# Four reordering casts of a weight matrix, shared among three engines instead of one

## The chip, the cores and the metric

The kernel runs on one core of a Trainium2 chip. The core has five engines with a queue of instructions each, run in order: PE (matrix multiply, with weight loads shown as PEld), ACT (ScalarE), DVE (VectorE), POOL (GpSimd) and SP (SyncE, which here only issues transfers). They work side by side and wait for each other through semaphores. The metric is the time of one execution on the device, in microseconds (us).

## The reference

A gated linear attention over 4 batches, 8 heads, 768 tokens and a head size of 48 gives `x` of 3072 tokens by 384; two matrix products with a gate between them follow.

```python
f = 1.0 / (1.0 + np.exp(-f_logit))
for t in range(S):
    state = f[:, :, t, :, None] * state + np.einsum('bhd,bhe->bhde', k[:, :, t], v[:, :, t])
    y[:, :, t] = np.einsum('bhd,bhde->bhe', q[:, :, t], state)
...
h = x @ w_in            # w_in: 384 x 2048
g = h * np.cos(h)
return (g @ w_out).astype(np.float32)   # w_out: 2048 x 384
```

Inputs and output are float32.

## The kernel before

**Two halves.** The attention is done in 12 pairs of 128-token chunks (256 tokens a pair, three pairs a batch). The products are done in 13 units `m` of tokens: units 0 and 1 have 128 tokens (together the first pair), the other eleven have 256. Unit 2 is the second pair.

**Steps of a pair `n`.** Loads `f`, `k`, `q`, `v` (SP, some ACT); `ex`, `ln`, `fx`, `fy` make decays from `f_logit` on ACT; `qa`, `ka`, `qm`, `km` scale q and k on POOL; `ad` adds two decays (POOL); `cum` sums them on PE and `eb`, `ei` take exponents on ACT; `vb` and `vt` lay out v; `tq`, `tk` turn q and k on PE and `qkt` copies them; `sc` are the scores (PE, L461), `am` masks them (DVE, L465); `ps`, `st`, `sz` carry the state (PE, DVE); `y` and `yi` are the outputs (PE, L535); `xe` copies each into `x` (ACT or DVE).

**Steps of a unit `m`.** `h{m}.{j}{s}` multiplies x by a part of w_in (PE, L583) into a pair of PSUM banks, `co{m}.{j}` takes the cosine on ACT (L588, its own activation table), `g{m}.{j}` multiplies the two on DVE (L565) into a tile `g`, `o{token tile}.{s}` multiplies `g` by a quarter of w_out (PE, L599), `ot` and `out` copy and store. A unit of 128 tokens has two `j`, one of 256 tokens four.

**The weights.** Each of w_in and w_out comes in four pieces of 768 KB. `w{part}.{i}` fetches a piece as float32 into a slot of the tile pool `g`, which is the same pool that the gates write to; `wc{part}.{i}` casts it to bf16 into its final place. For w_in (part 0) the cast also reorders: column 4n + r of a piece goes to place 128r + n, since w_out is fetched with four neighbouring rows on a partition (L281). Per partition that is 3 rows of 512 elements, 1536 in all. Each of the four casts reads one float out of four, with a step of 16 bytes, and writes in a row. The w_out casts copy in a row on both sides.

Slots of `g` set waits: w0.3 is fetched into the slot of w0.0, so it waits for wc0.0; w1.1 follows in the same slot and waits for wc0.3; w1.3 waits for wc1.1. The gates g1.* go to the slot of w0.1 and g2.* to that of w0.2, so they wait for wc0.1 and wc0.2. h0.00 and h1.00 need wc0.0; h1.01, h0.01 and h2.1* need wc0.1; h2.2*, h1.10 and h0.10 need wc0.2; h2.3*, h1.11 and h0.11 need wc0.3.

**Order.** Every engine's order comes from one list of words, `ORDER` (L36 to L117). `wc0.0:G` says that step wc0.0 runs on POOL at this place; T, S, V, G, Y stand for PE, ACT, DVE, POOL and SP, and numbers behind are the places of new tiles (of PSUM banks T0 to T7 for matmuls). Nothing is reordered later. ACT changes its activation table between the exponent group (L641) and the cosines (L588). The first 51 matmuls, by zeros (L264), stand among the first attention steps and write nothing that is used.

Of the kernel before, what the change touches and what calls it, by code (L numbers as in the profile page):

```python
# [15 lines left out]
B, H, S, D = 4, 8, 768, 48  # L16
# [14 lines left out]
         "sz": 4, "x": 4, "g": 5, "co": 4, "ot": 4}  # L31
WITHIN = 12
ZEROS = 51


ORDER = """  # L36
# [11 lines left out]
zf45:T4 vt0.3:S zf46:T0 qm1.0:V zf47:T1 zqk.0:V vb1:G1 cum3:T6 ka1.1:V tk1.0:T7 am0.1:V0 eb3:S1  # L48
tq1.0:T km1.1:G ps1.0:T0,1 qkt1.0:S3 zf48:T4 zf49:T4 zf50:T4 qa1.1:V ps1.1:T vt1.1:G2 vt1.3:S
sc1.0:T2 zsp.2:V qm1.1:V y0:T7 ex2:S st1.00:V q3:Y1 tq1.1:T4 am1.0:V0 tk1.1:T w0.2:Y3 ei3:S0 ln2:S0  # L50
qkt1.1:V4 wc0.0:G vt1.2:S sz1.00:V0 xe0.1:S0 st1.01:V xe0.0:S sz1.01:V sc1.1:T4 ad2:G2 w0.3:Y1
vt1.0:S yi1:T0,3 am1.1:V2 fx2:S k3:Y2 h0.00:T6 fy3:S w1.0:Y2 wc0.1:G cum2:T2 y1:T ei2:S1 xe1.0:S1
h1.00:T4 xe1.1:V qa3:G eb2:S0 h1.01:T st1.11:V st1.10:V qm3.1:G2 h2.00:T2 sz1.11:V3 sz1.10:V h0.01:T
co1.0:S2 qm3.0:G h2.01:T co0.0:S0 wc0.2:G q2:Y1 g1.0:V4 h2.11:T0 h2.10:T co2.0:S1 g0.0:V0 wc0.3:G
h2.20:T4 co2.1:S2 h2.21:T g2.0:V3 h1.10:T6 ka3:G w1.1:Y1 co2.2:S3 f5:Y2 h1.11:T g2.1:V km3.0:G fy2:S
h0.10:T2 k2:S0 h0.11:T wc1.0:G g2.2:V co1.1:S0 h2.31:T0 co0.1:S1 g1.1:V h2.30:T qa2:G w1.2:Y2
o0.0:T5 v2:Y0 co2.3:S3 zsz.2:V qm2.1:G1 g0.1:V o1.0:T6 o2.0:T4 qm2.0:G wc1.1:S g2.3:V tq3.1:T7
# [131 lines left out]
def describe(nc, cpool, ppool, q, k, v, f_logit, moe_w_in, moe_w_out, out):  # L189
    G = Graph()  # L190
    eng = lambda e: {"DVE": nc.vector, "POOL": nc.gpsimd, "ACT": nc.scalar, "SP": nc.sync}[e]

    def tl(shape, dt, name):
        return cpool.tile(shape, dt, name=name)

    def copy(e, o, i):
        (nc.scalar.copy if e == "ACT" else eng(e).tensor_copy)(out=o, in_=i)  # L197


    if ZEROS:  # L200
        zero = tl([128, 512], BF16, "zero")
# [57 lines left out]

    if ZEROS:  # L260
        for i in range(ZEROS):
            dump = Val(p1)
# [8 lines left out]
    def weights(part, i):  # L271
        dst, stage = (w_in_v, w_out_v)[part][i], Val(gS)
        w, cnt = ((512, KM), (DM, 4))[part]
        view = lambda: stage.ap.bitcast(F32).rearrange("p a n -> p (a n)")[:, 0:cnt * w].rearrange(
            "p (a n) -> p a n", n=w)

        def fetch(e):
            if part == 0:
                src = moe_w_in.rearrange("(km p) f -> p km f", p=128)[:, :, i * 512:(i + 1) * 512]
            else:  # L280
                src = moe_w_out.rearrange("(q p r) m -> q p r m", p=128, r=4)[i]  # L281
            eng(e).dma_start(out=view(), in_=src)
        G.step(f"w{part}.{i}", ("SP",), fetch, writes=[stage])


        def cast(e):
            if part == 0:
                copy(e, dst.ap.rearrange("p k (r n) -> p k r n", r=4), view().rearrange("p k (n r) -> p k r n", r=4))
            else:
                copy(e, dst.ap, view())  # L290
        G.step(f"wc{part}.{i}", ("POOL", "ACT"), cast,
               reads=[stage], writes=[dst])

    for part in range(2):
        for i in range(NQ):
            weights(part, i)
# [425 lines left out]
```

## Time and profile before

| | |
|---|---|
| Time, median of 3 runs | 185.94 us (185.43 to 186.01) |
| The profiled execution: time, and its span on the core | 186.08 us, 184.2 us |
| PE busy | 172.6 us (94% of the span) |
| DVE, ACT, POOL busy | 140.9, 128.6, 115.3 us |
| The four w_in casts on POOL (L197) | 12.0 us, first start 21.0, last start 33.9 |

Times in the trace are counted from the start of the span. A timeline row gives start, length, engine, line, operation, output and inputs with shapes, a count, and in brackets the idle time ahead of it with what ended it. All copies and casts share one helper line, L197, so they are told apart by their tiles. Neighbouring instructions of an engine overlap by up to 0.1 us in the rows, since one starts while the one before ends.

### The profile page before, as it was taken

The page shows a single profiled execution, that of the slowest core. Times are in us where ns is not written, and L with a number is a line of the kernel's source. Part 1 is how long each engine was busy: PE and PEld are TensorE (multiplying, and loading weights), DVE is VectorE, ACT ScalarE, POOL GpSimd, SP SyncE. Part 2 cuts the span into 40 slices and gives each one's busy share as a digit, 9 for nine tenths or more (in the row PEclk, how much of TensorE's full clock was granted, in tenths as well). Part 3 has the DMA queues.
Part 4 walks back from the last instruction along what each step waited for, and adds up shares of the span by engine and source line. Part 5 has one row for each costly group of instructions (what it writes and reads, how often), then busy time and mean ns, then how long its engine had stood idle before and what let it go on. Part 6 is the DMA issues. An engine that isn't in the chain of part 4 may idle for free.

```text
span 184.2 us, 5974 instructions
## 1 busy us (share of the span) xinstructions
PE 172.6 (94%) x2541; PEld 124.7 (68%) x2541; DVE 140.9 (77%) x214; ACT 128.6 (70%) x182; POOL 115.3 (63%) x136
## 2 busy tenths in 40 slices
PE   7999778498999999999999999999999999999991
PEld 2464467485667877688766886668877877776660
DVE  6379976774989799999999799879789986672110
ACT  5595888577967999997999989737961675343110
POOL 3069999999976999999928999999920000000000
PEclk9999999999999999999999999999999999999999
DMA  5999799499999999999999998941963100100233
GB/s 141 276 262 293 249 271 357 134 276 334 310 234 258 251 204 246 246 279 234 210 245 242 303 214 207 116 91 22 161 138 132 43 4 4 43 0 0 85 131 128
DMA packets 70746, 33.94 MB, mean 184 GB/s; under 512 B 65344, under 2 KB 68672, under 8 KB 70720
## 3 DMA queue, kind: packets, MB, share of 16 engines
q1 hardware_dynamic: 67680, 32.28, 72.9%
q10 hardware_dynamic: 3040, 1.28, 2.7%
q8 instruction: 20, 0.33, 0.8%
q14 instruction: 6, 0.05, 0.1%
HBM read 25.17 MB, written 4.72 MB: 162 GB/s over the span
## 4 chain that ended last, share of the span: by engine, by line
PE 80%; DMA 5%; POOL 5%; DVE 5%; issue 2%; ACT 1%; POOLq 0%; DVEq 0%
PE ps L599 34%; PE ps L583 29%; PE ps L264 5%; PE ps L535 4%; POOL w_in_bf L197 3%; DMA g<-in_moe_w_out_dram 3%; PE ps L461 3%; PE ps L483 2%; DMA q<-in_q_dram 2%; DVE am L465 1%; PE ps L441 1%; PE ps L381 1%; POOL qk L411 1%; ACT w_out_bf L197 1%; DVE sz L507 1%
## 5 line engine op out<-in xcount | busy, mean ns | idle before, releaser
L565 DVE TENSOR_TENSOR g<-ps,co 128x1024 bf16<-128x1024 f32 x48 | 60.6, 1308 | 13.6 <-ACT co L588 10.3
L583 PE MATMUL ps<-x,w_in_bf 128*128 128x256 bf16 (+1 forms) x624 | 67.0, 264 | 3.3 <-POOL w_in_bf L197 3.3
L599 PE MATMUL ps<-w_out_bf,g 128*128 128x384 bf16 x384 | 68.3, 326 | 0.5 <-ACT w_out_bf L197 0.5
L588 ACT ACTIVATE co<-ps,halfpi 128x1024 bf16<-128x1024 f32 x48 | 52.5, 1114 | 18.3 <-PE ps L583 17.1
L583 PEld LDWEIGHTS <-w_in_bf 128*128 128x128 bf16 x624 | 56.4, 98 | 12.0 <-POOL w_in_bf L197 3.9
L599 PEld LDWEIGHTS <-g 128*128 128x128 bf16 x384 | 36.0, 98 | 22.7 <-issue 0.7
L465 DVE TENSOR_TENSOR am<-ps,pmask 128x1024 bf16<-128x1024 f32 x24 | 28.6, 1218 | 2.3 <-PE ps L461 2.2
L411 POOL TENSOR_TENSOR qk<-k,bi 128x384 bf16<-128x384 f32 x22 | 21.8, 1002 | 1.3 <-DVE k L358 0.3
L411 POOL TENSOR_TENSOR qk<-q,b 128x384 bf16<-128x384 f32 x21 | 20.8, 1002 | 2.1 <-ACT f L354 1.5
L197 POOL COPY vt<-vb 64x384 bf16<-64x384 bf16 x36 | 18.3, 512 | 1.5
L197 ACT COPY ot<-ps 128x384 f32<-128x384 f32 (+1 forms) x13 | 5.9, 451 | 16.3 <-PE ps L599 11.1
L507 DVE TENSOR_TENSOR sz<-ps,b 64x192 bf16<-64x192 f32 x40 | 13.9, 354 | 2.5 <-PE ps L483 1.5
L264 PE MATMUL ps<-zero 128*128 128x512 bf16 x51 | 14.7, 435 | 1.2 <-DVE zero L203 1.2
L197 DVE COPY ot<-ps 128x384 f32<-128x384 f32 (+1 forms) x13 | 6.8, 523 | 9.6 <-ACT ot L197 5.2
L197 POOL CAST vb<-v 128x768 bf16<-128x768 f32 x10 | 8.6, 856 | 7.6 <-DMA v<-in_v_dram 6.9
L370 POOL TENSOR_TENSOR sp<-ls 128x384 bf16<-128x384 f32 x10 | 10.3, 1032 | 4.6 <-ACT ls L340 3.8
L501 DVE TENSOR_TENSOR ps<-ps,sz 64x192 f32<-64x192 f32 x32 | 11.6, 365 | 1.4 <-PE ps L483 0.5
L197 POOL CAST w_in_bf<-g 128x1536 bf16<-128x1536 f32 x4 | 12.0, 3026 | 0.1
L336 ACT ACTIVATE f<-f 128x768 f32<-128x768 f32 (+1 forms) x14 | 10.5, 749 | 1.7 <-DMA f<-in_f_logit_dram 1.7
L348 POOL TENSOR_TENSOR q<-f,q 128x384 f32<-128x384 f32 x10 | 10.0, 1004 | 1.4 <-DMA q<-in_q_dram 1.2
L461 PE MATMUL ps<-qkt 48*64 48x128 bf16 x384 | 9.2, 220 | 1.7 <-ACT x L197 1.7
L358 POOL TENSOR_TENSOR k<-k,f 128x384 f32<-128x384 f32 (+1 forms) x11 | 10.6, 963 | 0.3
(60 smaller groups left out, 162.4 us busy)
## 6 DMA issues: line engine op xcount, KB each, us to landing
v<-in_v_dram SPq DMA_DIRECT2D x12, 384.0 KB, 6.1
out_dram<-ot SPq DMA_DIRECT2D x22, 192.0 KB, 2.6
f<-in_f_logit_dram SPq DMA_DIRECT2D x10, 384.0 KB, 6.5
q<-in_q_dram SPq DMA_DIRECT2D x9, 384.0 KB, 5.4
k<-in_k_dram SPq DMA_DIRECT2D x9, 384.0 KB, 5.7
g<-in_moe_w_in_dram SPq DMA_DIRECT2D x4, 768.0 KB, 7.1
g<-in_moe_w_out_dram SPq DMA_DIRECT2D x4, 768.0 KB, 5.9
f<-in_f_logit_dram SPq DMA_DIRECT2D x4, 192.0 KB, 3.6
```

Of the source, the lines that this page charges most:

```text
L197: (nc.scalar.copy if e == "ACT" else eng(e).tensor_copy)(out=o, in_=i)
L264: G.step(f"zf{i}", ("PE",), lambda e, dump=dump: nc.tensor.matmul(dump.ap, lhsT=zero[:, 0:128], rhs=zero, start=True, stop=True), writes=[ ...
L358: eng(e).tensor_mul(out=w.ap[:, :, 0, :], in0=w.ap[:, :, 0, :], in1=t.ap[:, :, 0, :])
L411: G.step(f"{nm}{n}.{u}", ("POOL", "DVE") if cut else ("POOL",), lambda e, u=u, j=j, src=src, dec=dec: eng(e).tensor_mul(out=qkp[u][j].ap[: ...
L461: nc.tensor.matmul(o[t, r, 2 * a + g, :].rearrange("p (e n) -> p e n", e=2), lhsT=qkv(u)[s, 1, a, g, x, :], rhs=qkv(u)[s, 0, a, g, :, :], ...
L465: G.step(f"am{n}.{u}", ("DVE",), lambda e, u=u, sc=sc: nc.vector.tensor_mul(out=am[u].ap.rearrange("p r b n -> p (r b) n"), in0=sc.ap.rear ...
L501: nc.vector.tensor_add(out=view()[s], in0=view()[s], in1=S0.ap[s, :, r, :])
L507: eng(e).tensor_mul(out=new.ap[s, :, r, :].rearrange("p (u a) n -> p u a n", u=2), in0=view()[s].rearrange("p (u a) n -> p u a n", u=2), i ...
L565: nc.vector.tensor_mul(out=o.rearrange("p b (n e) -> p b e n", e=2), in0=ph.ap.rearrange("p (b e n) -> p b e n", e=2, n=64), in1=co.ap.rea ...
L583: nc.tensor.matmul(ph.ap[:, i * T:(i + 1) * T].rearrange("p (g t) -> p g t", t=C), lhsT=w_in_bf[:, kk, f0:f0 + 128], rhs=xa[:, :, kk, :], ...
L588: G.step(f"co{m}.{j}", ("ACT",), lambda e, ph=ph, co=co: nc.scalar.activation(out=co.ap, in_=ph.ap, func=AF.Sin, bias=halfpi), reads=[ph], ...
L599: nc.tensor.matmul(po.ap[:, 0:DM], lhsT=gT.ap[:, j, i * C:(i + 1) * C], rhs=w_out_bf[:, j, :], start=(po.first and j == 4 * s), stop=(po.f ...
```

## The change

Of the four w_in casts, wc0.0 and wc0.1 run on ACT, wc0.2 stays on POOL and wc0.3 runs on DVE, each at the place in the list where it stood. wc0.1 and wc0.2 are written the other way round: they read the floats in a row and write each of them 128 bf16 places (256 bytes) from the last. What is computed, and where it ends up, is the same; no other word of the list is changed.

```diff
+BY_ROWS = (1, 2)
...
-qkt1.1:V4 wc0.0:G vt1.2:S sz1.00:V0 xe0.1:S0 st1.01:V xe0.0:S sz1.01:V sc1.1:T4 ad2:G2 w0.3:Y1
-vt1.0:S yi1:T0,3 am1.1:V2 fx2:S k3:Y2 h0.00:T6 fy3:S w1.0:Y2 wc0.1:G cum2:T2 y1:T ei2:S1 xe1.0:S1
+qkt1.1:V4 wc0.0:S vt1.2:S sz1.00:V0 xe0.1:S0 st1.01:V xe0.0:S sz1.01:V sc1.1:T4 ad2:G2 w0.3:Y1
+vt1.0:S yi1:T0,3 am1.1:V2 fx2:S k3:Y2 h0.00:T6 fy3:S w1.0:Y2 wc0.1:S cum2:T2 y1:T ei2:S1 xe1.0:S1
...
-co1.0:S2 qm3.0:G h2.01:T co0.0:S0 wc0.2:G q2:Y1 g1.0:V4 h2.11:T0 h2.10:T co2.0:S1 g0.0:V0 wc0.3:G
+co1.0:S2 qm3.0:G h2.01:T co0.0:S0 wc0.2:G q2:Y1 g1.0:V4 h2.11:T0 h2.10:T co2.0:S1 g0.0:V0 wc0.3:V
...
             if part == 0:
-                copy(e, dst.ap.rearrange("p k (r n) -> p k r n", r=4), view().rearrange("p k (n r) -> p k r n", r=4))
+                at = "p k n r" if i in BY_ROWS else "p k r n"
+                copy(e, dst.ap.rearrange(f"p k (r n) -> {at}", r=4), view().rearrange(f"p k (n r) -> {at}", r=4))
             else:
                 copy(e, dst.ap, view())
-        G.step(f"wc{part}.{i}", ("POOL", "ACT"), cast,
+        G.step(f"wc{part}.{i}", ("POOL", "ACT", "DVE"), cast,
```

Line numbers grow by one, and from the cast on by two, so L197 is L198 afterwards and L588 is L590. ACT's queue around the first copies of x, before: behind ln2 (L340) stand vt1.2, xe0.1, xe0.0, vt1.0, fx2, fy3, ei2, xe1.0, eb2 and the table load ahead of the cosines.

```order
L340 ACTIVATE ls_109<-f_94 128x768
L197 COPY vt_125<-vb_121 64x8x48
L197 COPY x_139<-ps_160 128x384
L197 COPY x_139<-ps_161 128x384
L197 COPY vt_125<-vb_121 64x8x48
L354 ACTIVATE f_94<-ls_109 128x8x48
L351 ACTIVATE f_95<-f_95 128x8x48
L402 ACTIVATE bi_115<-ps_159 128x384
L197 COPY x_140<-ps_158 128x384
L402 ACTIVATE b_111<-ps_159 128x392
L588 ACT_TABLE_LOAD
```

The same place on ACT after the change:

```order
L342 ACTIVATE ls_109<-f_94 128x768
L198 COPY w_in_bf<-g_144 128x3x512
L198 COPY vt_125<-vb_121 64x8x48
L198 COPY x_139<-ps_160 128x384
L198 COPY x_139<-ps_161 128x384
L198 COPY vt_125<-vb_121 64x8x48
L356 ACTIVATE f_94<-ls_109 128x8x48
L353 ACTIVATE f_95<-f_95 128x8x48
L198 COPY w_in_bf<-g_147 128x3x128x4
L404 ACTIVATE bi_115<-ps_159 128x384
L198 COPY x_140<-ps_158 128x384
L404 ACTIVATE b_111<-ps_159 128x392
```

wc0.0 now stands ahead of both copies of x, and wc0.1 (whose output shape 128x3x128x4 shows the writing steps) between fy3 and ei2.

DVE's queue at the first gates, before (g1.0, g0.0, three gates of unit 2, g1.1):

```order
L507 TENSOR_TENSOR sz_138<-ps_158,b_113 64x4x48 x2
L565 TENSOR_TENSOR g_147<-ps_160,co_150 128x8x2x64
L565 TENSOR_TENSOR g_143<-ps_161,co_148 128x8x2x64
L565 TENSOR_TENSOR g_146<-ps_159,co_149 128x8x2x64
L565 TENSOR_TENSOR g_146<-ps_158,co_150 128x8x2x64
L565 TENSOR_TENSOR g_146<-ps_160,co_151 128x8x2x64
L565 TENSOR_TENSOR g_147<-ps_161,co_148 128x8x2x64
```

and after:

```order
L509 TENSOR_TENSOR sz_138<-ps_158,b_113 64x4x48 x2
L567 TENSOR_TENSOR g_147<-ps_160,co_150 128x8x2x64
L567 TENSOR_TENSOR g_143<-ps_161,co_148 128x8x2x64
L198 COPY w_in_bf<-g_144 128x3x512
L567 TENSOR_TENSOR g_146<-ps_159,co_149 128x8x2x64
L567 TENSOR_TENSOR g_146<-ps_158,co_150 128x8x2x64
L567 TENSOR_TENSOR g_146<-ps_160,co_151 128x8x2x64
```

wc0.3 stands behind the second gate and ahead of the next six.

## The prediction

> **What bounds the kernel now.** I read the page's first part and its chain first, to see which engine sets the end; then a table of stages, to see where that engine idles; then the chain in order of time; and last the timelines of the engines that the change touches, in the stage where the four casts run.
>
> The page of the kernel before:
> ```profile
> span 184.2 us, 5974 instructions
> PE 80%; DMA 5%; POOL 5%; DVE 5%; issue 2%; ACT 1%; POOLq 0%; DVEq 0%
> ```
> Stages of 5 us (stage, its length, then busy time of PE, PEld, DVE, ACT, POOL, granted clock, DMA):
> ```profile
> 20.00:25.00 5.00, 2.90 (x115) 2.12 (x114) 4.90 (x11) 4.90 (x11) 4.87 (x4) 1.00 0.72 221
> 25.00:30.00 5.00, 4.22 (x92) 3.79 (x89) 2.71 (x6) 4.00 (x7) 4.92 (x4) 1.00 0.96 307
> 30.00:35.00 5.00, 3.26 (x33) 2.71 (x31) 3.57 (x3) 3.28 (x4) 5.00 (x4) 1.00 0.88 275
> 35.00:40.00 5.00, 4.24 (x63) 3.92 (x62) 3.87 (x4) 3.46 (x4) 4.92 (x4) 1.00 0.63 156
> 40.00:45.00 5.00, 4.23 (x37) 2.74 (x35) 3.65 (x5) 3.56 (x4) 4.92 (x6) 1.00 1.05 354
> 45.00:50.00 5.00, 5.00 (x85) 3.36 (x83) 3.60 (x5) 4.85 (x7) 4.67 (x7) 1.00 1.05 310
> ```
> PE is full from 45 us on. Whatever comes earlier or later at 45 us moves the end by as much. Before that PE idles, POOL is full, and ACT and DVE have some 30% free, though not between 20 and 25 us, where both are at 4.90 of 5.00. The chain in order of time (start, length, what) shows what carries PE into the full stretch:
> ```profile
> 31.09 5.82 POOL w_in_bf L197 x2
> ...
> 36.92 5.88 DMA g<-in_moe_w_out_dram
> ...
> 42.83 1.48 ACT w_out_bf L197
> ...
> 44.35 1.46 PE ps L599 x8
> ```
> The last two casts of w_in end on POOL at 36.9; that frees the staging buffer into which SP fetches the second piece of w_out (w1.1, 5.88 us); ACT casts it (wc1.1), and PE starts o0.1 at 44.35. From 36.90 (the end of wc0.3) to 44.35 this is 7.45 us of fixed work. The DMA queue's own waits say the same:
> ```profile
> SPq L282 <- POOL w_in_bf L197: 6.8, 2, 5.3
> ```
> The PE timeline has the direct waits:
> ```profile
> 23.80 0.42 PE L461 MATMUL ps<-qkt 48*64 48x128 bf16 x16 [1.73 <-ACT x L197]
> 26.54 0.84 PE L583 MATMUL ps<-x,w_in_bf 128*128 128x128 bf16 x12
> 28.16 4.13 PE L583 MATMUL ps<-x,w_in_bf 128*128 128x128 bf16 x48 [0.78 <-POOL w_in_bf L197]
> 34.04 2.15 PE L583 MATMUL ps<-x,w_in_bf 128*128 128x256 bf16 x24 [1.74 <-POOL w_in_bf L197]
> 36.95 3.49 PE L583 MATMUL ps<-x,w_in_bf 128*128 128x128 bf16 x48 [0.76 <-POOL w_in_bf L197]
> 44.35 1.46 PE L599 MATMUL ps<-w_out_bf,g 128*128 128x384 bf16 x8 [0.54 <-ACT w_out_bf L197]
> ```
> So the casts do bound this stage, by 3.3 us of direct waits. The question is when the last of them ends under the change.
>
> **What a stepping cast costs.** Groups of instructions of one shape (count, busy us, mean ns):
> ```profile
> L197 ACT CAST w_out_bf<-g 128x1536 bf16<-128x1536 f32 x2 | 2.9, 1464 | 1.2 <-DMA g<-in_moe_w_out_dram 1.2
> L197 ACT CAST vb<-v 128x768 bf16<-128x768 f32 x2 | 1.7, 830 | 0.0
> L197 POOL CAST w_in_bf<-g 128x1536 bf16<-128x1536 f32 x4 | 12.0, 3026 | 0.1
> L197 POOL CAST w_out_bf<-g 128x1536 bf16<-128x1536 f32 x2 | 2.9, 1465 | 0.1
> L197 DVE COPY ot<-ps 128x384 f32<-128x384 f32 x11 | 6.1, 553 | 4.4 <-PE ps L599 4.2
> L197 DVE COPY ot<-ps 128x192 f32<-128x192 f32 x2 | 0.7, 358 | 5.2 <-ACT ot L197 5.2
> L197 DVE COPY qkt<-ps 128x1024 bf16<-128x1024 bf16 x8 | 5.4, 678 | 2.4 <-PE ps L441 2.4
> ```
> On POOL the same 1536 elements cost 1465 ns in a row and 3026 ns when they are read four floats apart: a factor of 2.07. No row shows ACT or DVE doing this, on either side.
>
> ACT, called S below: the low end is its dense cast, 1.46; the high end is that times POOL's factor, 3.02. I take 2.73: the two dense ACT rows give (1464 - 830) / 768 = 0.826 ns per element and 195 ns fixed, and doubling the element part alone gives 195 + 2 x 1269 ns. It is nearest the one stepping row that there is, and both ACT casts touch memory at every step at least 16 bytes on, one reading, one writing. [...]
>
> DVE, called D: the two copies of ot give 1.016 ns per element, so 1.72 us for 1536 at one element a step; the qkt row, 678 ns for 1024 two-byte elements, scaled by 1.5 gives a low end of 1.02; 1.72 times 2.07 gives a high end of 3.56. I take 1.72, between them. POOL's writing cast (wc0.2) lies between 1.47 and 3.03.
>
> **The change, step by step.** POOL first, with what it does now:
> ```profile
> 21.05 3.20 POOL L197 CAST w_in_bf<-g 128x1536 bf16<-128x1536 f32 x1
> 25.12 2.99 POOL L197 CAST w_in_bf<-g 128x1536 bf16<-128x1536 f32 x1
> 28.05 1.01 POOL L348 TENSOR_TENSOR q<-f,q 128x384 f32<-128x384 f32 x1
> 29.14 1.95 POOL L411 TENSOR_TENSOR qk<-q,b 128x384 bf16<-128x384 f32 x2
> 31.04 5.86 POOL L197 CAST w_in_bf<-g 128x1536 bf16<-128x1536 f32 x2
> ```
> It loses three casts, about 9 us. ACT, from where wc0.0 goes in:
> ```profile
> 22.86 0.51 ACT L197 COPY vt<-vb 64x384 bf16<-64x384 bf16 x1
> 23.28 0.84 ACT L197 CAST x<-ps 128x384 bf16<-128x384 f32 x2
> 24.99 0.51 ACT L351 ACTIVATE f<-f 128x384 f32<-128x384 f32 x1
> 26.08 0.49 ACT L402 ACTIVATE bi<-ps 128x384 f32<-128x384 f32 x1 [0.59 <-PE ps L387]
> 26.83 0.52 ACT L402 ACTIVATE b<-ps 128x392 f32<-128x392 f32 x1
> 27.36 1.28 ACT L588 ACT_TABLE_LOAD   x1
> 29.05 1.11 ACT L588 ACTIVATE co<-ps,halfpi 128x1024 bf16<-128x1024 f32 x1 [0.40 <-PE ps L583]
> ```
> and DVE's first two gates, behind which wc0.3 goes in:
> ```profile
> 30.25 2.59 DVE L565 TENSOR_TENSOR g<-ps,co 128x1024 bf16<-128x1024 f32 x2 [1.47 <-issue]
> ```
> 1. wc0.0 starts on ACT at 22.86 and the six instructions behind it start S - 0.09 later (neighbours overlap by 0.09: 22.86 + 0.51 against 23.28). Its data are there, since POOL read them at 21.05. The casts of x are among the six: PE's scores, released by them at 23.80, go to 26.44. PE recovers only the 0.29 us or so of small waits behind them, so the block at 26.54, the last ahead of w0.1's first use, ends near 29.8.
> 2. wc0.1 follows fy3, which ended at 25.50: it starts at 25.32 + S and ends at 25.32 + 2S = 30.78. PE's block of 48 starts there and not at 28.16, 2.6 us late.
> 3. Behind wc0.1 on ACT stand ei2, xe1.0, eb2, the table load and co1.0; from wc0.1's end to the end of the two gates it is -0.09 + 0.75 + 0.53 + 1.28 + 1.11 + 0.09 + 2.59 = 6.26 us, with the two PE waits (0.59 and 0.40) gone. The gates end at 37.04, against 32.84 now.
> 4. wc0.2 on POOL is hidden: q3's product follows fy3 (28.1), the two qm steps end at 31.1, the cast by 34.2 at the dearest. PE can't begin h2.20 before the first gate frees its PSUM bank at 35.7. Without that cover it would cost its lateness in full. POOL's 9 us buy nothing: the next waits are for ACT and DVE.
> 5. wc0.3 on DVE ends at 37.04 + D = 38.76; the fetch of w0.3 waits for wc0.0 at 25.50 in place of 24.25, 1.25 late, and has until 37. Now it is 36.90. So w1.1 is asked for 1.86 us later; with the 7.45 us, o0.1 starts at 46.2.
> 6. Queued behind wc0.3 on DVE are six gates. The fifth frees the bank of tq3.0, which stands before o0.1 on PE: 38.76 + 5 x 1.30 (half of 2.59) = 45.3, and then some 0.8 us of transposes: 46.1. This second path ends at the same place, so a faster fetch alone would not win it back. SP's fetches behind w1.1 (f5, w1.2) no longer wait for a late POOL, and hide.
>
> The sum against the profiled execution, 186.08 us (span 184.2 and 1.88 around it): 186.08 + 1.86 = 187.94. The median of the runs, 185.94, is 0.14 lower, so 187.8. In general the shift is 25.32 + 2S + 6.26 + D - 36.90 = 2S + D - 5.32.
>
> **Rivals.**
> - *ACT steps at its dense price* (faster). S = 1.46 gives 2.92 + 1.72 - 5.32 = -0.68: 185.3, and with D = 1.02 184.6. For it: POOL's factor may be POOL's own. Against it: that row is the only evidence on steps. With D = 1.72 it decides below S = 1.80.
> - *Only one side of stepping costs on ACT.* One cast at 2.73, one at 1.46: 4.19 + 1.72 - 5.32 = +0.59, 186.5, at the edge of what counts as slower. That two casts now step in writing would do what it is for, by half.
> - *Dear steps everywhere*: S = 3.02, D = 3.56 give +4.28, 190.2. Against it: DVE would have to pay POOL's factor on top of its slowest rate.
> - *PE loses its clock.* The gap before the scores, 22.07 to 23.80 now, grows to 26.44: 4.4 us. The rows show 1.00 through 1.73 us of waiting, and nothing longer. At half clock the block of 48 would take 8.26 us in place of 4.13, and its third quarter, which co0.0 needs, would end at 30.78 + 6.20 = 36.98, 2.7 us after co0.0's turn at 34.27. If the clock came back half-way through that, 1.35 us would be left: 187.8 + 1.35 = 189.2. [...]
>
> **How the numbers follow.** Both ACT casts pay: 0.46. Clock on top: 0.07. Dear steps everywhere: 0.05. One side pays: 0.16, half of it within the bound. Dense price: 0.26. A measurement here tells changes over 0.3% (0.56 us) from none. Slower: 0.46 + 0.07 + 0.05 + 0.05 = 0.63; same: 0.11 and a little of the dense case, 0.12; faster: 0.25. The likeliest case alone goes from S = 2.5 with D = 1.02 (+0.7, 186.6) to S = 2.9 with D = 2.6 (+3.1, 189.0). The range reaches down to the dense case at 185.0, and up to 189.6, short of the dearest corners.
>
> **What would show it.** In the profile after: the two w_in casts on ACT near 2.7 us each; PE's scores waiting some 4.4 us for x; the wait for w_in_bf moved from POOL to ACT; the first gate near 34.5; wc0.3 ending near 38.8, and o0.1 starting near 46.2. I am wrong if the ACT casts measure under 1.8 us, or if wc0.3 ends late and o0.1 does not.

## The result, and the profile after

The changed kernel takes 192.75 us (median of 3 runs, 192.72 to 193.52) against 185.94 us before: a ratio of 1.0388, with an interval of 1.0339 to 1.0436. The direction was forecast, the size was not: 187.8 us with a range of 185.0 to 189.6 had been given, and the loss is 6.8 us instead of 1.9.

The profiled execution took 193.52 us, its span is 191.3 us. From ACT's timeline after (start, length, engine, line, operation, output and inputs, count, and in brackets the idle time ahead), from wc0.0 to the first two cosines:

```profile
22.92 2.90 ACT L198 CAST w_in_bf<-g 128x1536 bf16<-128x1536 f32 x1
...
26.26 0.84 ACT L198 CAST x<-ps 128x384 bf16<-128x384 f32 x2
...
28.39 7.04 ACT L198 CAST w_in_bf<-g 128x1536 bf16<-128x1536 f32 x1
...
37.80 1.11 ACT L590 ACTIVATE co<-ps,halfpi 128x1024 bf16<-128x1024 f32 x1
```

The first row is wc0.0, which reads with steps: 2.90 us. The row of 7.04 us is wc0.1, which writes with steps. Both handle the same 1536 elements a partition. The timelines of POOL and of DVE show the other two:

```profile
31.54 7.01 POOL L198 CAST w_in_bf<-g 128x1536 bf16<-128x1536 f32 x1
```
```profile
38.95 1.32 DVE L567 TENSOR_TENSOR g<-ps,co 128x1024 bf16<-128x1024 f32 x1 [6.12 <-ACT co L590]
40.69 1.33 DVE L567 TENSOR_TENSOR g<-ps,co 128x1024 bf16<-128x1024 f32 x1 [0.42 <-ACT co L590]
41.90 2.00 DVE L198 CAST w_in_bf<-g 128x1536 bf16<-128x1536 f32 x1
43.82 4.88 DVE L567 TENSOR_TENSOR g<-ps,co 128x1024 bf16<-128x1024 f32 x4
```

wc0.2, the other writing cast, costs 7.01 us on POOL, so it is the direction and not the engine that is dear. DVE waits 6.12 us for the first cosine, its first gate starts at 38.95 instead of 30.25, and wc0.3 ends at 43.90 instead of 36.90. PE's timeline after:

```profile
26.78 0.64 PE L463 MATMUL ps<-qkt 48*64 48x128 bf16 x16 [4.53 <-ACT x L198]
...
35.48 9.32 PE L585 MATMUL ps<-x,w_in_bf 128*128 128x128 bf16 x84 [4.05 <-ACT w_in_bf L198]
45.17 2.81 PE L585 MATMUL ps<-x,w_in_bf 128*128 128x128 bf16 x36 [0.37 <-DVE g L567]
47.82 2.40 PE L601 MATMUL ps<-w_out_bf,g 128*128 128x384 bf16 x12
50.05 1.06 PE L443 MATMUL ps<-ident,qk 128*128 128x128 bf16 x16
50.95 1.46 PE L601 MATMUL ps<-w_out_bf,g 128*128 128x384 bf16 x8
```

o0.1, the last row, starts at 50.95; before, it started at 44.35. So 6.6 of the 7.4 us between the two profiled executions exist by then. The other 0.8 us lie behind it. From o0.1's start to the end of the last L601 (L599) matmul it is 137.0 us after and 136.1 us before, and in the kernels below whose profile is used to its end it lies between 136.1 and 137.0 us, though all have the same work there; that part was not followed up. Some runs of a kernel are slower than its others, so the ratios compare the quicker runs alone, and of three profiles taken in a slower run (the held clock, POOL alone writing, and two casts on DVE) only the stretch up to o0.1 is used.

The chain in order of time shows the same path:

```profile
23.02 2.80 ACT w_in_bf L198
...
28.48 6.95 ACT w_in_bf L198
...
35.48 4.04 PE ps L585 x30
...
39.54 1.12 ACT co L590
...
40.69 1.19 DVE g L567
...
41.90 2.01 DVE w_in_bf L198
...
43.93 4.81 DMA g<-in_moe_w_out_dram
```

Before, POOL's casts stood here. Now ACT's two casts carry 9.75 us of it. In the table of stages the clock column (the first figure behind POOL's) is no longer 1.00 everywhere:

```profile
25.00:30.00 5.00, 3.22 (x64) 2.67 (x67) 1.23 (x1) 4.95 (x8) 1.36 (x2) 0.68 0.94 314
30.00:35.00 5.00, 1.43 (x44) 1.15 (x44) 2.00 (x5) 5.00 (x2) 5.00 (x3) 0.84 0.97 308
35.00:40.00 5.00, 4.52 (x34) 3.97 (x35) 1.05 (x1) 4.34 (x7) 4.92 (x3) 0.50 0.02 4
```

Three things had to be told apart: what writing with steps costs by itself, which of the two writing casts carries the loss, and what the halved clock adds.

### The profile page after: what moved, and what is told of

The parts are those of the page before. It is cut to its first block, busy times and chain, and to the rows that moved or that the text cites. A ratio compares the mean times of both kernels' runs of the same rounds, so it can differ in the third digit from the quotient of the medians.

```text
span 191.3 us, 5974 instructions
## 1 busy us (share of the span) xinstructions
PE 176.6 (92%) x2541; PEld 127.9 (67%) x2541; DVE 141.5 (74%) x215; ACT 138.4 (72%) x184; POOL 110.3 (58%) x133
## 2 busy tenths in 40 slices
DMA packets 70746, 33.94 MB, mean 177 GB/s; under 512 B 65344, under 2 KB 68672, under 8 KB 70720
## 4 chain that ended last, share of the span: by engine, by line
PE 69%; ACT 13%; DVE 5%; DMA 5%; issue 3%; POOL 3%; POOLq 0%; DVEq 0%; ACTq 0%
PE ps L585 30%; PE ps L601 25%; ACT w_in_bf L198 5%; PE ps L265 5%; PE ps L537 4%; DMA g<-in_moe_w_out_dram 3%; DMA f<-in_f_logit_dram 2%; ACT f L338 2%; PE ps L463 2%; POOL qk L413 2%; PE ps L485 1%; ACT ls L342 1%; ACT co L590 1%; PE ps L443 1%; DVE w_in_bf L198 1%
## 5 line engine op out<-in xcount | busy, mean ns | idle before, releaser
L585 PE MATMUL ps<-x,w_in_bf 128*128 128x256 bf16 (+1 forms) x624 | 70.0, 272 | 4.6 <-ACT w_in_bf L198 4.0
L601 PE MATMUL ps<-w_out_bf,g 128*128 128x384 bf16 x384 | 68.4, 326 | 0.1
L585 PEld LDWEIGHTS <-w_in_bf 128*128 128x128 bf16 x624 | 58.8, 102 | 13.8 <-ACT w_in_bf L198 4.2
L590 ACT ACTIVATE co<-ps,halfpi 128x1024 bf16<-128x1024 f32 x48 | 52.7, 1114 | 16.8 <-PE ps L585 15.7
L601 PEld LDWEIGHTS <-g 128*128 128x128 bf16 x384 | 35.9, 98 | 22.2 <-issue 0.3
L198 POOL COPY vt<-vb 64x384 bf16<-64x384 bf16 x36 | 18.1, 505 | 1.5
L198 ACT COPY ot<-ps 128x384 f32<-128x384 f32 (+1 forms) x13 | 5.9, 450 | 16.3 <-PE ps L601 16.1
L198 DVE COPY ot<-ps 128x384 f32<-128x384 f32 (+1 forms) x13 | 6.8, 523 | 10.2 <-ACT ot L198 5.2
L198 POOL CAST vb<-v 128x768 bf16<-128x768 f32 x10 | 8.9, 895 | 8.7 <-DMA v<-in_v_dram 7.8
L463 PEld LDWEIGHTS <-qkt 48*64 48x64 bf16 x384 | 6.6, 108 | 7.0 <-issue 4.2
```

Source lines behind the costliest of these rows:

```text
L463: nc.tensor.matmul(o[t, r, 2 * a + g, :].rearrange("p (e n) -> p e n", e=2), lhsT=qkv(u)[s, 1, a, g, x, :], rhs=qkv(u)[s, 0, a, g, :, :], ...
L585: nc.tensor.matmul(ph.ap[:, i * T:(i + 1) * T].rearrange("p (g t) -> p g t", t=C), lhsT=w_in_bf[:, kk, f0:f0 + 128], rhs=xa[:, :, kk, :], ...
L590: G.step(f"co{m}.{j}", ("ACT",), lambda e, ph=ph, co=co: nc.scalar.activation(out=co.ap, in_=ph.ap, func=AF.Sin, bias=halfpi), reads=[ph], ...
L601: nc.tensor.matmul(po.ap[:, 0:DM], lhsT=gT.ap[:, j, i * C:(i + 1) * C], rhs=w_out_bf[:, j, :], start=(po.first and j == 4 * s), stop=(po.f ...
```

## The experiments

Since the start of the span varies against the work, o0.1 is counted below from the start of the first L537 (L535) block of chunk outputs behind the score mask, which comes ahead of all four casts and starts between 20.16 and 21.40 in the profiles below. These are its rows before and after:

```profile
20.83 0.63 PE L535 MATMUL ps<-am,vt 128*32 128x128 bf16 x32
```
```profile
21.01 0.63 PE L537 MATMUL ps<-am,vt 128*32 128x128 bf16 x32
```

On this scale o0.1 stands at 23.53 before and at 29.94 after: +6.41. The ratios of the experiments go with runs of the kernel before on the same chip, whose medians were 187.0 to 187.6 us there.

### What a stepping cast costs by itself

In this kernel (m1_steps_alone in later texts) 1536 elements a partition are copied on one engine after the other, one pattern at a time. Four of the twelve patterns (name, output type, size, the view written, the view read; rstepb reads a float out of four, weight and whundred write bf16 places 16 and 256 bytes apart, fsixtyfour writes floats 256 bytes apart):

```python
def rows(t): return t.rearrange("p (k n) -> p k n", k=3)
def outs(t, r): return rows(t).rearrange("p k (r n) -> p k n r", r=r)
def wide(t, r): return rows(t).rearrange("p k (n r) -> p k n r", r=r)
def across(t, r): return rows(t).rearrange("p k (n r) -> p k r n", r=r)   # reads() is the same
...
("rstepb", BF16, 1536, lambda o: outs(o, 4).rearrange("p k n r -> p k r n"), lambda s: reads(s, 4)),
("weight", BF16, 1536, lambda o: across(o, 8), lambda s: rows(s).rearrange("p k (r n) -> p k r n", r=8)),
("whundred", BF16, 1536, lambda o: outs(o, 4), lambda s: wide(s, 4)),
("fsixtyfour", F32, 1536, lambda o: outs(o, 8), lambda s: wide(s, 8)),
```

> This kernel leaves the whole computation out; it only runs casts of 1536 elements on a partition, one at a time on ScalarE, then GpSimd, then VectorE, with other steps on the reading or the writing side, and last one cast that writes by 256 bytes on ScalarE and GpSimd at once. Theory A (a write to a far place is dear in itself): the cast that writes by 256 bytes (whundred) takes about 7.0 us on ScalarE and on GpSimd when nothing else runs, and the pair at the end the same. Theory B (the two writing casts slowed each other, or the transfers slowed them): about 2.9 us alone, and near 7 in the pair. Theory C (256 bytes is a bad step, since it always meets the same bank): 7 at 256 bytes but about 3 at 272 bytes (wodd). Reading four floats apart (rstepb): 2.90 on ScalarE, 2.98 on GpSimd, 2.0 on VectorE, as in the two profiles.

Some of its groups of instructions (the letter ahead of a name is the engine: s ACT, g POOL, v DVE):

```profile
L61 ACT CAST s_whundred_x<-src 128x1536 bf16<-128x1536 f32 x1 | 7.3, 7302 | 0.0
L63 POOL CAST g_whundred_x<-src_s_x 128x1536 bf16<-128x1536 f32 x1 | 7.2, 7219 | 0.0
L63 DVE CAST v_whundred_x<-src_g_x 128x1536 bf16<-128x1536 f32 x1 | 7.2, 7216 | 0.0
L61 ACT CAST s_weight_x<-src 128x1536 bf16<-128x1536 f32 x1 | 7.0, 7035 | 0.0
L61 ACT CAST s_wfour_x<-src 128x1536 bf16<-128x1536 f32 x1 | 3.6, 3577 | 0.0
L61 ACT COPY s_fsixtyfour_x<-src 128x1536 f32<-128x1536 f32 x1 | 3.1, 3078 | 0.0
L61 ACT CAST s_rstepb_x<-src 128x1536 bf16<-128x1536 f32 x1 | 2.9, 2879 | 0.0
L61 ACT CAST s_dense_x<-src 128x1536 bf16<-128x1536 f32 x1 | 1.5, 1471 | 3.2 <-DMA src<-in_moe_w_in_dram 3.2
```

The rows are ACT's but for the first three, which show the same pattern on each engine. All three engines, in ns:

| pattern | ACT | POOL | DVE |
|---|---|---|---|
| in a row on both sides | 1471 | 1463 | 961 |
| reading floats 8 bytes apart | 1533 | 1536 | 1735 |
| reading floats 16 bytes apart | 2879 | 2872 | 2835 |
| reading floats 32 bytes apart | 2931 | 2927 | 2882 |
| writing bf16 4 bytes apart | 1882 | 1882 | 1836 |
| writing bf16 8 bytes apart | 3577 | 3588 | 3531 |
| writing bf16 16 bytes apart | 7035 | 6997 | 6999 |
| writing bf16 256 bytes apart | 7302 | 7219 | 7216 |
| writing bf16 272 bytes apart | 7087 | 6996 | 6991 |
| writing floats 256 bytes apart | 3078 | 2991 | 2981 |

The 7 us are the price of the pattern itself, alone on an otherwise idle core (theory A). That casts slow each other, or are slowed by transfers, falls with it (B): ACT and POOL writing at the same time took 7014 and 7190 ns. That 256 bytes is an unlucky step falls too (C): 16 bytes is as dear, and 272 is no cheaper. At 256 bytes apart, writing two-byte elements costs about 2.4 times what writing four-byte elements costs, on all three engines (7216 to 7302 against 2981 to 3078 ns). The forecast of 2.0 us for DVE's reading cast missed: it took 2.84 here, which the last experiment takes up.

### Both writing casts turned back

Against the kernel after:

```diff
-BY_ROWS = (1, 2)
+BY_ROWS = ()
```

> The changed kernel with the same engines, but all four casts step on the reading side. The prediction's own formula with the measured reading prices, 2 x 2.90 + 2.00 - 5.32 = +2.48, gives 188.4; the matmul clock may still halve once behind the 4.5 us gap ahead of the scores, which adds 0 to 0.8. If the writing side is not what made the change cost 6.8, it stays near 192.7.

Measured: 188.83 us, ratio 1.0096 (1.0064 to 1.0129). Its timelines of ACT and of PE, with wc0.1 and with o0.1 (46.49 - 20.50 = 25.99, +2.46):

```profile
22.41 2.89 ACT L198 CAST w_in_bf<-g 128x1536 bf16<-128x1536 f32 x1
...
27.86 2.97 ACT L198 CAST w_in_bf<-g 128x1536 bf16<-128x1536 f32 x1
```
```profile
46.49 1.46 PE L601 MATMUL ps<-w_out_bf,g 128*128 128x384 bf16 x8
```

The casts take 2.89 and 2.97 us on ACT, 2.93 on POOL and 2.60 on DVE. Of the +6.41 at o0.1 the writing side is thus 3.95, and placing the casts on ACT and DVE the other 2.46. This is the kernel that the forecast's price described. It was forecast as 1.9 us slower, and it is about 1.8 (0.0096 of the 187.2 us that the kernel before took beside it). That the two are so close is partly luck: all three moved casts were dearer than forecast, and o0.1 came 2.46 us later.

### One writing cast at a time

```diff
-BY_ROWS = (1, 2)
+BY_ROWS = (1,)
```

> The changed kernel, but wc0.2 on GpSimd steps in reading again; only wc0.1 on ScalarE writes by steps. Theory (the ScalarE writing cast alone carries the loss, GpSimd's 7 us lie beside it): o0.1 starts 29.5 to 30.0 us after y0's first matmul, as in the changed kernel (29.9), and the ratio to the kernel before stays at 1.033 to 1.039. Rival (both writing casts carry it): the ratio falls to about 1.025.

```diff
-BY_ROWS = (1, 2)
+BY_ROWS = (2,)
```

> The changed kernel, but wc0.1 on ScalarE steps in reading again; only wc0.2 on GpSimd writes by steps, 7.0 us in place of 2.9. Theory: with ScalarE early again, GpSimd's cast ends near 38 and is now the last thing that h2.2 and the gates of unit 2 wait for, in part beside wc0.3 on VectorE; 0 to 1.5 us above the all-reading kernel (ratio 1.0096), so 1.010 to 1.018, and far below 1.0388. Rival (a writing cast costs its 4.1 us wherever it stands): 1.032.

With ACT alone writing: 192.47 us, ratio 1.0316 (1.0261 to 1.0372), just below the end of the expected 1.033 to 1.039. The count starts at 20.39 there, and o0.1 stands at 29.92, the same as with both (29.94):

```profile
50.31 1.46 PE L601 MATMUL ps<-w_out_bf,g 128*128 128x384 bf16 x8
```

Up to o0.1, ACT's wc0.1 therefore carries the whole extra loss, and POOL's wc0.2 adds nothing to it. But POOL's cast is only covered by ACT's lateness. With POOL alone writing, the comparison gives 1.0185 (1.0118 to 1.0252) and o0.1 stands at 27.43, 1.44 later than with no writing cast. PE's timeline there:

```profile
30.42 5.33 PE L585 MATMUL ps<-x,w_in_bf 128*128 128x128 bf16 x60
38.16 7.13 PE L585 MATMUL ps<-x,w_in_bf 128*128 128x256 bf16 x72 [2.41 <-POOL w_in_bf L198]
```

PE waits 2.41 us for POOL's cast of 31.07 to 38.11, a wait that the kernel after doesn't show.

### The writing side without any move

All four casts stay on POOL, where they were before; only wc0.1 and wc0.2 write with steps. Against the kernel before:

```diff
+BY_ROWS = (1, 2)
...
+at = "p k n r" if i in BY_ROWS else "p k r n"
```

> One part of the change alone: all four casts on GpSimd as before, wc0.1 and wc0.2 stepping on the writing side. Theory (each writing cast costs 4.05 us more and nothing hides GpSimd there): wc0.3 ends 8.1 us later and the time rises by about 8, to 195 (ratio 1.04 to 1.05). Rival (GpSimd has slack): ratio below 1.02.

Measured: 194.36 us, ratio 1.0411 (1.034 to 1.0482), two runs only. POOL's four casts took 3.18, 7.02, 7.04 and 3.02 us and o0.1 stands at 31.26, +7.73. PE's timeline has both waits:

```profile
32.64 6.46 PE L585 MATMUL ps<-x,w_in_bf 128*128 128x128 bf16 x48 [4.84 <-POOL w_in_bf L198]
42.28 2.15 PE L585 MATMUL ps<-x,w_in_bf 128*128 128x256 bf16 x24 [3.18 <-POOL w_in_bf L198]
```

So the writing side alone makes the kernel as slow as the whole change does: the two ratios can't be told apart. At o0.1 the move to three engines wins 1.32 of the 7.73 us back.

### The clock kept up

Two groups of matmuls by zeros, 14 and 18, go ahead of the two waits of PE in the kernel after; they write banks that are not read:

```diff
-sz1.01:V sc1.1:T4
+sz1.01:V zg0:T4 sc1.1:T4
...
-eb2:S0 h1.01:T
+eb2:S0 zg1:T3 h1.01:T
```

> The changed kernel with 32 matmuls by zeros put into the two gaps of PE (14 ahead of the second scores, 18 ahead of h1.01), so that PE is never idle for 3 us there; nothing else differs. If the halved clock (35 to 40 us, and 26 to 30 us) only ran beside the waits, the time falls by 0.3 to 0.5 us, to about 192.3. If the clock is a large part of the loss, it falls by 1.5 us or more, to 191.2 or below. Either way the granted clock should stay at 1.00 between 25 and 45 us.

The stages of that kernel, the three that stood at 0.68, 0.84 and 0.50:

```profile
25.00:30.00 5.00, 4.93 (x110) 3.47 (x110) 2.66 (x5) 4.95 (x8) 2.18 (x3) 1.00 0.92 277
30.00:35.00 5.00, 3.46 (x21) 1.55 (x20) 0.56 (x2) 5.00 (x3) 5.00 (x2) 1.00 0.80 261
35.00:40.00 5.00, 4.45 (x51) 3.84 (x48) 1.87 (x2) 4.97 (x7) 4.92 (x4) 1.00 0.01 2
```

The clock stayed at 1.00, and o0.1 stands at 29.58 against 29.94: 0.36 us earlier. The comparison, 1.0352 (1.0276 to 1.0428), can't be told from the change's own. By these two profiles the halved clock is real and costs about 0.36 of the 6.41 us; PE waits for ACT and DVE in most of that stretch anyway.

### Only VectorE helps, and reads

From the kernel before, one cast alone goes to DVE, on the reading side. First wc0.2, ahead of the first gate (e3_v_second in the texts below):

```diff
-wc0.2:G q2:Y1 g1.0:V4
+wc0.2:V q2:Y1 g1.0:V4
```

> The kernel before with one cast moved: wc0.2 runs on VectorE ahead of its first gate, reading by steps; the other three stay on GpSimd, reading by steps. VectorE waits there now from 28.8 to 30.2, the data of w0.2 land at 28.9, the cast takes 2.0 as measured: the first gate starts 0.7 us later, but wc0.3 on GpSimd ends 2.9 us earlier (34.0). Theory (the end of the last cast sets o0.1): o0.1 comes 1.5 to 2.9 us earlier, 183.0 to 184.4 us. Rival (VectorE's gates then set it, or GpSimd and VectorE block each other): 185 to 186.5.

then wc0.3, where the change had put it (e7_v_last):

```diff
-g0.0:V0 wc0.3:G
+g0.0:V0 wc0.3:V
```

> The other part alone: wc0.3 on VectorE behind its second gate, reading by steps; the other three on GpSimd, reading by steps. Theory (the stepping cast on VectorE takes 2.0 us and VectorE and GpSimd shut each other out, as the pair of qm steps did beside the VectorE cast in e3, 3.03 us for 1.95): it can't start before wc0.2 ends on GpSimd at 34.0, ends at 36.0, and o0.1 comes 0.5 to 0.9 us earlier; ratio 0.993 to 0.997. Rival (no lock): it starts at 32.9, ends at 34.9, o0.1 comes 1.9 us earlier; ratio 0.990.

then both:

```diff
-wc0.2:G q2:Y1 g1.0:V4 h2.11:T0 h2.10:T co2.0:S1 g0.0:V0 wc0.3:G
+wc0.2:V q2:Y1 g1.0:V4 h2.11:T0 h2.10:T co2.0:S1 g0.0:V0 wc0.3:V
```

> Only wc0.2 and wc0.3 run on VectorE (reading side, ahead of the first gate and behind the second), wc0.0 and wc0.1 stay on GpSimd. From e3_v_second and e7_v_last: wc0.2 ends near 32.1; the first gate starts there, the two gates end near 34.7; wc0.3 follows at 2.0 to 2.5 us and ends near 36.9, where it ends now; GpSimd is late by the stretch of qm (1.1 us) but has 6 us less to do. Theory (the end of wc0.3 alone sets o0.1): o0.1 within 0.5 us of before, ratio 0.995 to 1.003, worse than e7_v_last because two casts in one queue add where one on each engine overlap. Rival (POOL being free matters too): GpSimd's later steps come 3 us sooner, wc1.1 and w1.2 come sooner and the ratio is as in e7_v_last or below, 0.985 to 0.992.

| on DVE | median, us | ratio to before (interval) | o0.1 (before 23.53) |
|---|---|---|---|
| wc0.2 | 185.44 | 0.991 (0.9866 to 0.9955) | 23.07 |
| wc0.3 | 185.63 | 0.9912 (0.9874 to 0.995) | 22.20 |
| wc0.2 and wc0.3 | 186.74 | 0.991 (0.9866 to 0.9954) | 23.43 |

The first two are faster than both kernels, by about 1% against the kernel before, with intervals that leave out 1. With wc0.2 there, the theory missed at o0.1: 0.46 us earlier and not 1.5 to 2.9, though the medians of the runs lie 1.73 us apart (185.44 and 187.17). In that profile POOL's first cast waited 1.54 us for its data, and POOL then works without a gap up to wc0.3:

```profile
22.14 2.97 POOL L198 CAST w_in_bf<-g 128x1536 bf16<-128x1536 f32 x1 [1.54 <-DMA g<-in_moe_w_in_dram]
```

It starts 1.38 us behind the count's start there and 0.22 before, so the 0.46 may understate the gain. The timeline of DVE with wc0.3 there:

```profile
31.53 2.51 DVE L567 TENSOR_TENSOR g<-ps,co 128x1024 bf16<-128x1024 f32 x2 [1.09 <-issue]
33.94 2.46 DVE L198 CAST w_in_bf<-g 128x1536 bf16<-128x1536 f32 x1
```

wc0.3 ends at 36.40 there, 15.0 us behind the count's start against 16.07 before, and o0.1 gains 1.33, between the 0.5 to 0.9 of the theory and the 1.9 of the rival; the ratio's interval holds parts of both. The gates end at 34.04 there, so the cast's start at 33.94 doesn't tell whether POOL held it back. The third is not shown to gain: its profile has o0.1 where it was before, its median over all runs is 186.74 against 187.0, and its runs spread from 183.86 to 188.24, so the 0.991 of the table, though in the rival's range, is weak evidence. Its DVE casts add up in one queue, as the theory had it (wc0.3 ends at 37.68):

```profile
30.28 2.16 DVE L198 CAST w_in_bf<-g 128x1536 bf16<-128x1536 f32 x1
32.36 2.50 DVE L567 TENSOR_TENSOR g<-ps,co 128x1024 bf16<-128x1024 f32 x2
34.74 2.94 DVE L198 CAST w_in_bf<-g 128x1536 bf16<-128x1536 f32 x1
```

### DVE's cast, and POOL beside it

DVE's stepping cast took 2.00 us in the kernel after and 2.84 us alone, and POOL's work beside it ran late (with wc0.2 on DVE, 3.03 us for the two qm steps in place of 1.95). The same reading cast on DVE into three separate rows of 512 (gap_x, as in the kernel) and into one row of 1536 (flat_x), first alone and then while POOL does ten casts of 768:

```python
nc.vector.tensor_copy(out=gap[:, :, 0:512].rearrange("p k (r n) -> p k r n", r=4), in_=four)   # gap: 128 x 3 x 640
nc.vector.tensor_copy(out=flat.rearrange("p (k r n) -> p k r n", k=3, r=4), in_=four)          # flat: 128 x 1536
```

> The whole computation is left out: only VectorE's reading-side cast (1536 floats read 16 bytes apart) is done, once into three separate rows of 512 (gap_x, as the kernel's own cast writes) and once into one row of 1536 (flat_x, as in m1_steps_alone), each alone and then each while GpSimd has ten casts of 768 in its queue. Open from the kernels: VectorE's cast took 2.00 us there and 2.83 in m1_steps_alone, and GpSimd's work beside it ran 1.1 us late. [...] Theory Q (the form does not matter, the kernel's 2.00 comes from something else, such as which banks are used): both forms 2.83 alone, and GpSimd keeps 0.75 us a cast beside both. Theory R (the form matters, the blocking is by any stepping): gap_x 2.0, flat_x 2.83, and GpSimd stretched beside both.

Its timeline on DVE (alone: the first two rows; beside POOL: the last two), then POOL's row in the middle of the last gap_x cast, and POOL's ten as one line (ns, least, median, most):

```profile
5.41 1.96 DVE L30 CAST gap_x<-src 128x1536 bf16<-128x1536 f32 x1 [5.41 <-DMA src<-in_moe_w_in_dram]
7.27 2.85 DVE L33 CAST flat_x<-src 128x1536 bf16<-128x1536 f32 x1
...
15.99 2.89 DVE L33 CAST flat_x<-src 128x1536 bf16<-128x1536 f32 x1
...
18.79 2.38 DVE L30 CAST gap_x<-src 128x1536 bf16<-128x1536 f32 x1
```
```profile
19.49 1.55 POOL L46 CAST busy_x<-farther_x 128x768 bf16<-128x768 f32 x1
```
```profile
L46 POOL CAST busy_x<-farther_x x10: 827/827/1547, 15.7 to 24.7; 128x768 bf16<-128x768 f32 x10
```

The form decides: three rows on both sides take 1.96 us, one row 2.85, so theory Q falls. Beside flat_x POOL's casts keep to the median of 827 ns, but for its first (1.01 us), which starts beside another DVE copy; the cast that falls beside gap_x takes 1547, and gap_x itself 2.38 in place of 1.96. POOL is stretched beside one form and not beside the other, so R falls too. The 0.42 us that gap_x lost and the 0.72 us that POOL's cast lost come to less than gap_x's own 1.96. Why the form decides, and how the two engines slow each other, no run here shows.

## Why the prediction was right about the direction and wrong about the size

**The step that failed is the price of wc0.1 on ACT**, in the part on what a stepping cast costs, and with it step 2. One value S = 2.73 stood for both ACT casts, "one reading, one writing", with 3.02 as the high end. The reading one measured 2.90, inside these bounds. The writing one measured 7.04, more than twice the high end. The bounds came from POOL's row, which is a reading cast with floats; no row of the profile before showed two-byte elements written far apart, and the high end should have been marked as holding for the reading side only. Neither of the two signs of being wrong that the prediction named came up; a cast dearer than the high end was not among them.

**The formula held for wc0.3's end, within 0.3 us.** With the measured prices in place of 2S + D, the shift of wc0.3's end is 2.90 + 7.04 + 2.00 - 5.32 = +6.62. The trace has it at 43.90 - 21.01 = 22.89 on the experiments' scale against 36.90 - 20.83 = 16.07, so +6.82. With ACT alone writing the sum is 2.90 + 7.03 + 1.99 - 5.32 = +6.60, and o0.1 shifts by 6.39. With no writing cast it is 2.89 + 2.97 + 2.60 - 5.32 = +3.14, where wc0.3's end shifts by 2.86 and o0.1 by 2.46.

Point by point:

1. wc0.0 on ACT and the scores: right. The scores waited 4.53 us for x (4.4 were forecast) and started at 26.78 (26.44).
2. wc0.1's end was forecast at 30.78 and came at 35.43. Of these 4.65 us the prices of the two casts are 4.48, and the other 0.18 is the later start of the work in this span (21.01 against 20.83). The wait of PE moved from POOL to ACT as said: 4.05 us.
3. From wc0.1's end to the end of the two gates 6.26 us were forecast. It took 42.02 - 35.43 = 6.59. Here the clock is a part: the 30 matmuls before co0.0 were still at half speed, and DVE waited 0.42 us for it.
4. "wc0.2 on POOL is hidden", by 34.2 at the dearest: the price was wrong again (7.01 us, end at 38.55). The cover that it named, the first gate, still hides it, but only because ACT's lateness moves that gate's end to 40.27; with ACT's wc0.1 reading, wc0.2 costs 1.44 us at o0.1.
5. wc0.3 on DVE took 2.00 us, between the two ends named (1.02 and 3.56) and 0.28 above the value taken. Behind its end the 7.45 us became 7.05: the fetch took 4.81 us in place of 5.88, and then a cosine on ACT (to 49.13) and PE's own queue took back some of what that won.
6. The second path, through PE's own queue, ended 0.4 us behind the first: ACT's cast of w1.1 runs from 49.07 to 50.54, and PE is busy until o0.1 at 50.95.

**The rivals.** The dense price and the price for one side alone fall: the reading side measured nearly double, the writing side nearly five times the dense 1.47. "Dear steps everywhere" had the right idea for the wrong cast: DVE was cheap (2.00 us). "PE loses its clock" named something that does happen (half clock at 26.8 to 30.2 and at 33.6 to 40.4 us) and put 1.35 us on it. No run shows that term, an estimate of the author's for a clock that falls to half and comes back half-way through the block; in the trace of before the granted clock is 0.50 only from 183.4 us on, behind the last matmul. Keeping the clock up changed o0.1 by 0.36.

**The width of the step.** For reading, 8 bytes apart is nearly free on ACT (1533 against 1471 ns), and 16 bytes apart, the step of POOL's row, pays (2879). For writing, closer places cost already: with bf16 4 bytes apart the cast takes 1882 ns, 8 bytes apart 3577, and 16 bytes apart 7035. The estimate rested on the nearest row, and that was a row of the other direction.

## What to carry to other kernels

When a cast must reorder, step on the side with the wider elements: 1536 floats read 16 bytes apart cost 2.8 to 2.9 us on every engine here (in the kernel's form on DVE 1.96 alone and 1.99 to 2.94 in the kernels), 1536 bf16 written as far apart 7.0. A bound drawn from the nearest row is a bound only for that row's direction and element size; where the edit changes either, its price is unknown until a single instruction has been measured. And here work moved off a full engine bought time only where the receiving engine was idle at that moment: ACT was at 4.90 of 5.00 there, and with two casts moved to it (and one to DVE) o0.1 came 2.5 us later even on the reading side, while one cast on DVE, put where DVE has a gap, won about 1%.

## What the hardware showed that was not expected

- Writing two-byte elements 16 to 272 bytes apart took 4.6 to 4.8 ns an element (6991 to 7302 / 1536) on ACT, POOL and DVE alike, and four-byte elements 256 bytes apart 1.9 to 2.0 (2981 to 3078 / 1536). Why two bytes are dearer than four was not tried.
- In the kernel after, the clock was halved for 3.41 us (26.78 to 30.19) and for 6.83 us (33.60 to 40.43): the first time from the end of PE's wait of 4.53 us on, the second time from within its wait of 4.05 us on. A halved clock came beside shorter waits too. In the run with wc0.2 on DVE, PE waited 1.89 us for x and the clock was halved from 24.86 to 28.28; in the profile of before, 1.73 us of waiting at the same place left it at 1.00, and with wc0.3 on DVE, where PE waited 1.72 us, it was halved from 24.16 to 27.58. What decides it, no run here shows. These times are from the trace's records of the granted clock; the table of stages of that last kernel agrees (2.58 of the second 5 us at half speed give 0.74):

```profile
20.00:25.00 5.00, 3.20 (x103) 2.06 (x92) 4.93 (x10) 4.90 (x9) 4.87 (x4) 0.92 0.61 188
25.00:30.00 5.00, 4.92 (x105) 4.42 (x103) 2.83 (x6) 3.30 (x7) 4.92 (x4) 0.74 0.93 280
```

- DVE's stepping cast and POOL's work can slow each other: with wc0.2 on DVE the two qm steps on POOL took 3.03 us in place of 1.95, with wc0.3 there the next POOL step took 1.89 in place of 1.00, and in the kernel of the two forms DVE's gap_x took 2.38 beside POOL in place of 1.96. A plan that counts such a DVE cast as free work beside POOL has to add these.
